# Attention with a gated MLP: score tiles by keys, one batch turned as 4-byte words on VectorE, two-bank accumulators, and the order of the work written anew

## The chip, the cores and the metric

The kernel runs on one core of a Trainium2 chip. The core has five engines that run at the same time, each through its own list of instructions in order: TensorE (PE, matrix products, which write to the PSUM accumulators), VectorE (DVE), ScalarE (ACT), GpSimd (POOL) and SyncE (SP). A weight load of the PE (PEld) overlaps its matmuls. Transfers (DMAs) run beside the engines; POOL and SP issue them. PSUM has eight banks of 2 KB for each of 128 partitions, so that one bank holds 512 fp32 columns. The metric is the time of one execution on the device, in microseconds (us), the median of several.

## The reference

Four batches of attention with eight heads, 768 positions and 64 columns a head. A query sees the 128 newest positions up to itself, and the first four positions (the sinks). The attention result, 768 x 512 per batch, goes through a gated block: a product with `w_in` and gelu give u and v of 512 columns each, v is normalised over its columns, mixed over the positions by the 768 x 768 matrix `w_sg`, and multiplied with u; a product with `w_out` is added to the attention result.

```
scores = q @ k.T / sqrt(64)
keep   = (key < 4) | ((query - key >= 0) & (query - key < 128))
x      = softmax(where(keep, scores, -1e9)) @ v          # heads side by side: (4, 768, 512)
h      = gelu(x @ w_in);  u, v = h[:, :512], h[:, 512:]
v_n    = (v - mean(v)) / sqrt(var(v) + 1e-6) * g_ln
v_s    = w_sg @ v_n + b_sg[:, None]                      # over positions, per batch
out    = x + (u * v_s) @ w_out
```

Inputs and output are fp32; the products run in bf16.

## The kernel before

Positions are cut into six tiles of 128, heads into four pairs. The whole work is a list of named steps, `STEPS`, written out in the kernel. Each step issues a few instructions; each engine carries out its own in the order of the list, and waits by semaphores for what it needs. No planner runs when the kernel is built: where a step stands in the list is what sets the order on every engine and on every DMA queue. A name carries the batch first, then a pair of heads, a tile, a half or a part, and a last letter where an engine can be chosen (A for ACT, D for DVE, P for POOL).

The steps of one batch, with their lines:

- **Loads.** Batch 0's q and k come as fp32 by SP (`LPQ`, `LPK`, L243, 384 KB each) and are cast by `CPQ`, `CPK`; those of the other batches come by POOL, cast on the way to bf16 (`LQ`, `LK`, L223, 128 KB each, six of either per batch). v comes in halves (`LVH`, L269, 384 KB), as do `w_in` (`LW`, L275, 512 KB) and `w_sg` (`LWS`, L280, 576 KB); then `w_out` (`LWO`, L283) and `b_sg` (`LB`, L299).
- **Turning q and k.** A score product needs q and k with the head's columns on the partitions. `HOW = "GBBC"` says how each batch is turned: batch 0 (G) and batches 1 and 2 (B) by PE transposes (`TQ`, `TK`, L371 and L377), read out by ACT or DVE (`EQ`, `EK`, L197, L198); batch 3 (C) by transposing DMAs from SP (`DQ`, `DK`, L435).
- **Scores.** `QK` (L478) makes one tile for a pair of heads and two tiles of queries, 2g and 2g + 1: for each of the pair's heads one matmul of 256 columns and one or two of 128, contraction 64. In a few steps of batch 0 a bias for the window is added by a matmul (L473). `EX` (L483) takes the exponential on ACT, `MK` multiplies by the window's mask on DVE (L490) or selects on POOL (L493, L496).
- **Sinks.** `KS`, `SK` and `SX` (L445, L457, L462) make the exponentials of the four sink positions, in two pieces for each batch.
- **Values.** `AV` (L519, L523, L526) makes, for one pair and two tiles (batch 0) or three tiles (the others) of queries, the products with v and with a column of ones in one PSUM bank; `NR` takes reciprocals of the sums (L535) and multiplies (L536). That is 36 such steps.
- **Block.** `XT`, `XE` (L545, L552; `XD` is the same as a DMA) turn x; `MV`, `GV` (L561, L565) make v and its gelu; `BN`, `RS`, `NM`, `Z` (L574 to L595) normalise it, where `RS` is a power on POOL (L583); `MU`, `GU` (L602, L607) make u. `WT`, `WE` (L614) turn `w_sg` once.
- **Gate and end.** `SP` (L622) multiplies with `w_sg` for one half of the positions and 128 columns, `GT` (L627) scales and adds `b_sg` on DVE, `GM` (L632) multiplies with u on DVE or POOL, `OU` (L639) multiplies with `w_out`, `RA` (L643) adds x on DVE, `ST` (L662) stores 128 rows, 24 times.

PSUM is used as two rings: two score tiles of two banks (`sc`), and four tiles of one bank (`mm`), each handed out in rotation. At the start, filler matmuls (`HM`, L188) run while the first loads come in. ACT loads a table of functions when it goes from exponentials to gelu and back.

Of the kernel before, what the change touches and what calls it, by code (L numbers as in the profile page):

```python
# [8 lines left out]
F32 = mybir.dt.float32  # L9
# [5 lines left out]
HOW = "GBBC"  # L15
VHOW = "HHHH"
# [4 lines left out]
WARM LPQ.0 FILL LPK.0 LPK.1 LPQ.1 LPQ.2 LG MASK LPK.2 LPK.3 CPQ.0.A VSK LPQ.3 IDEN CPK.0.A IDEN2 MASK0 HM.9 TQ.0.0  # L21
TK.0.0 EQ.0.0.D EK.0.0.A VSO HM.3 QK.0.0.0 ZERO CPK.1.P QK.0.0.1.1 EX.0.0.0 LVH.0.0 EX.0.0.1 QK.0.0.2.1 CPQ.1.D TK.0.1
EX.0.0.2 LC CPQ.2.D LVH.0.1 TQ.0.1 MK.0.0.0.D EK.0.1.A TQ.0.2 EQ.0.1.D EQ.0.2.A HM.2 QK.0.1.0 CPK.2.A CPK.3.P
QK.0.1.1.1 EX.0.1.0 LQ.1.0 CPQ.3.D TK.0.2 EX.0.1.1 TK.0.3 EK.0.2.D LQ.1.1 TQ.0.3 EK.0.3.A GTR EQ.0.3.D LW.0 QK.0.2.0
QK.0.2.1 EX.0.2.0 LK.1.0 KS.0 VSM.0 SK.0.2 EX.0.2.1 SK.0.1 MK.0.2.0.D AV.0.0.0 LW.1 QK.0.3.0.1 MK.0.1.0.D SX.0.1
SX.0.2 QK.0.3.1 MK.0.2.1.P GCP.D NR.0.0.0 EX.0.3.0 AV.0.0.1 AV.0.1.0 AV.0.1.1 NR.0.0.1 EX.0.3.1 QK.0.1.2 NR.0.1.0
AV.0.2.0 AV.0.3.0 EX.0.1.2 MK.0.3.1.P NR.0.1.1 QK.0.2.2 AV.0.2.1 NR.0.2.0 EX.0.2.2 TQ.1.0 NR.0.3.0 MK.0.1.2.P QK.0.3.2
AV.0.3.1 EQ.1.0.A NR.0.2.1 XT.0.0 NR.0.3.1 LWS.0 AV.0.0.2 EX.0.3.2 AV.0.1.2 XE.0.0.D LK.1.1 XT.0.1 MK.0.2.2.D MV.0.0
XE.0.1.A LK.1.2 NR.0.0.2 MK.0.3.2.D LK.1.3 NR.0.1.2 AV.0.2.2 AV.0.3.2 LQ.1.2 NR.0.2.2 GV.0.0 MV.0.1 NR.0.3.2 LQ.1.3
BN.0.0 LWS.1 XT.0.2 GV.0.1 MU.0.1 XE.0.2.A BN.0.1 WT.0 GU.0.1 TK.1.0 MV.0.2 RS.0.1 EK.1.0.A LK.1.4 NM.0.1 WE.0.A WT.1  # L30
GV.0.2 LK.1.5 TK.1.1 MU.0.2 LB.P EK.1.1.A BN.0.2 Z.0.0.A LK.2.0 WT.2 GU.0.2 MU.0.0 WE.1.D RS.0.2 WE.2.D Z.0.1.A LQ.2.0
NM.0.2 Z.0.2.A Z.0.3.D Z.0.4.D WT.3 LQ.2.1 WT.4 GU.0.0 WE.3.D WT.5 LQ.1.4 Z.0.5.D TQ.1.1 QK.1.0.0 EQ.1.1.D QK.1.1.0
# [34 lines left out]
ST.3.5  # L67
"""

HOLDS = ""


@with_exitstack
def kernel(
# [148 lines left out]
    def LQ(b, i):  # L225
        return load(q16, q, b, i)
# [484 lines left out]
```

## Time and profile before

Three runs took 156.59 to 156.99 us, median 156.65. The profiled execution has a span of 155.8 us, from its first to its last instruction, so that 0.85 us of the median lie around the span.

| | busy us | share of the span | instructions |
|---|---|---|---|
| PE, matmuls | 147.2 | 94% | 1543 |
| PEld, weight loads | 95.0 | 61% | 1543 |
| DVE | 123.0 | 79% | 295 |
| ACT | 98.9 | 63% | 110 |
| POOL | 99.7 | 64% | 127 |

Transfers moved 24.67 MB, of which the queue issued by POOL (software) moved 11.01 MB and SP's 13.41 MB. POOL's loads of batch 0's v landed 8.9 and 10.0 us after their issue, those of `w_in` 9 to 11 us; a store landed 2.3 us after its issue.

A row of the groups names line, engine and operation, output and inputs, shapes and a count, then the busy time and the mean of one in ns. The chain of work that ended last is followed back from the last instruction; a piece of it has a start, a duration and what it is. In a table by stage each row is a stretch of time. A duration in these views is that of one instruction on its engine; since matmuls are pipelined, the step from one to the next in a dense stretch of the chain is shorter than the duration of one.

### The profile page before, as it was taken

The numbers are of one execution on the slowest core, as the hardware profiler recorded it, in microseconds if no ns is written. First come the engines' busy times: TensorE is split into PE (matmuls) and PEld (weight loads), VectorE is DVE, ScalarE is ACT, GpSimd is POOL, SyncE is SP. The second block draws the span as 40 slices with busy tenths as digits, with TensorE's granted clock in tenths as the row PEclk, the third lists the DMA queues.
The fourth block names the chain that finished last, engine by engine and source line by source line (L and its number), as shares of the span: only waits on it lengthen the run. The fifth ranks groups of instructions, "written<-read, shape, count | busy, mean of one in ns | idle before, by whom it ended". The sixth has DMA issues, their size and how long they took to land.

```text
span 155.8 us, 3844 instructions
## 1 busy us (share of the span) xinstructions
PE 147.2 (94%) x1543; PEld 95.0 (61%) x1543; DVE 123.0 (79%) x295; ACT 98.9 (63%) x110; POOL 99.7 (64%) x127
## 2 busy tenths in 40 slices
PE   6998799999999999989999999999999999999990
PEld 2455487779775776747566764486567644876530
DVE  4576688829989989769789887899689956867981
ACT  3689789799989856276897855269954025591000
POOL 4099669578999899999559869640798610300400
PEclk9999689999999999999999999999999999999999
DMA  5899999999999999999999299995710580510064
GB/s 162 277 369 155 152 194 163 170 186 200 141 144 145 188 157 169 148 152 156 155 227 235 68 279 177 181 192 47 248 72 6 99 236 0 202 64 9 0 230 176
DMA packets 86170, 24.67 MB, mean 158 GB/s; under 512 B 78660, under 2 KB 83016, under 8 KB 86152
## 3 DMA queue, kind: packets, MB, share of 16 engines
q0 software_dynamic: 64608, 11.01, 97.1%
q1 hardware_dynamic: 21544, 13.41, 32.1%
q8 instruction: 12, 0.20, 0.5%
q14 instruction: 6, 0.05, 0.1%
HBM read 24.81 MB, written 6.29 MB: 200 GB/s over the span
## 4 chain that ended last, share of the span: by engine, by line
PE 75%; DMA 15%; DVE 2%; POOL 2%; issue 1%; ACT 1%; SPq 1%; ACTq 0%
PE mm L622 17%; PE sc L561 13%; PE mm L639 13%; PE sc L602 12%; DMA k<-in_k_dram 6%; DMA v_sb<-in_v_dram 6%; PE sc L478 5%; PE mm L519 4%; DMA uT<-in_k_dram 4%; PE mm L377 3%; PE mm L523 3%; PE mm L526 2%; PE mm L614 1%; PE mm L545 1%; DVE P L490 1%
## 5 line engine op out<-in xcount | busy, mean ns | idle before, releaser
L483 ACT ACTIVATE P<-sc 128x1024 bf16<-128x1024 f32 (+1 forms) x48 | 43.5, 956 | 10.9 <-PE sc L478 10.8
L622 PE MATMUL mm<-wsgT,z 128*128 128x384 bf16 x192 | 34.1, 327 | 0.0
L622 PEld LDWEIGHTS <-z 128*128 128x128 bf16 x192 | 17.7, 98 | 11.9 <-issue 0.7
L561 PE MATMUL sc<-w_in_sb,xT 128*128 128x512 bf16 x96 | 22.2, 379 | 0.7 <-ACT vt L565 0.7
L639 PE MATMUL mm<-w_out_sb,wsg_gated 128*128 128x512 bf16 x96 | 22.7, 379 | 0.0
L493 POOL TENSOR_SCALAR_AFFINE_SELECT P<-P 128x512 bf16<-128x512 bf16 x21 | 14.0, 665 | 13.3 <-ACT P L483 13.0
L627 DVE SCALAR_TENSOR_TENSOR gtmp<-mm,g_sb,b_bc 128x384 bf16<-128x384 f32 x32 | 19.1, 610 | 4.2 <-PE mm L622 3.6
L602 PE MATMUL sc<-xT,w_in_sb 128*128 128x256 bf16 x192 | 22.1, 273 | 0.0
L632 POOL TENSOR_TENSOR wsg_gated<-gtmp,uT 128x384 bf16<-128x384 bf16 x15 | 14.9, 1005 | 10.9 <-DVE gtmp L627 10.9
L574 DVE BATCH_NORM_STATS2 st<-vt 128x6 f32<-128x512 f32 x24 | 15.4, 684 | 7.5 <-ACT vt L565 7.4
L602 PEld LDWEIGHTS <-w_in_sb 128*128 128x128 bf16 x192 | 18.7, 98 | 3.0
L536 DVE TENSOR_TENSOR x_sb<-mm,rcp 128x384 bf16<-128x384 f32 (+1 forms) x36 | 18.5, 513 | 1.2
L565 ACT ACTIVATE vt<-sc 128x1024 f32<-128x1024 f32 x12 | 12.3, 1027 | 9.0 <-PE sc L561 8.9
L519 PE MATMUL mm<-v_sb,P 128*128 128x65 bf16 x192 | 16.8, 198 | 1.0 <-DMA v_sb<-in_v_dram 0.9
L643 DVE TENSOR_TENSOR ot<-mm,x_sb 128x512 f32<-128x512 f32 x24 | 16.1, 683 | 2.0 <-PE mm L639 1.9
L583 POOL TENSOR_TENSOR rs<-rs,neg_half 128x4 f32<-128x4 f32 (+1 forms) x8 | 7.0, 869 | 16.4 <-DVE rs L578 15.0
L519 PEld LDWEIGHTS <-P 128*128 128x128 bf16 x192 | 15.1, 100 | 2.9 <-issue 1.5
L223 POOL DMA_DIRECT2D q<-in_q_dram x18 | 16.7, 949 | 0.0
L223 POOL DMA_DIRECT2D k<-in_k_dram x18 | 16.4, 924 | 0.5 <-POOL wsg_gated L632 0.5
L523 PE MATMUL mm<-v_sb,P 128*128 128x65 bf16 x160 | 16.1, 197 | 0.0
L561 PEld LDWEIGHTS <-xT 128*128 128x128 bf16 x96 | 9.2, 98 | 10.9 <-issue 0.9
L478 PE MATMUL sc<-qT,kT 64*128 64x128 bf16 (+1 forms) x256 | 15.1, 242 | 0.6 <-ACT P L483 0.3
(90 smaller groups left out, 238.0 us busy)
## 6 DMA issues: line engine op xcount, KB each, us to landing
out_dram<-ot SPq DMA_DIRECT2D x24, 256.0 KB, 2.3
v_sb<-in_v_dram POOLq DMA_DIRECT2D x8, 384.0 KB, 8.5
q<-in_q_dram POOLq DMA_DIRECT2D x18, 128.0 KB, 6.3
k<-in_k_dram POOLq DMA_DIRECT2D x18, 128.0 KB, 6.5
wsg_gated<-in_moe_w_sg_dram POOLq DMA_DIRECT2D x2, 576.0 KB, 7.5
w_in_sb<-in_moe_w_in_dram POOLq DMA_DIRECT2D x2, 512.0 KB, 10.1
uT<-in_q_dram SPq DMA_DIRECT2D x2, 384.0 KB, 3.1
uT<-in_k_dram SPq DMA_DIRECT2D x2, 384.0 KB
```

The costliest lines, as they stand in the source:

```text
L223: return nc.gpsimd.dma_start(out=dst.rearrange("p (h d) -> p h d", h=H), in_=heads(src, b, i))
L478: nc.tensor.matmul(sc[:, hl, c:c + 128 * ni], at(kT, b)[rows, j, p, :], at(qT, b)[rows, i:i + ni, p, :], start=not biased, stop=(not biase ...
L483: nc.scalar.activation(out=P.new((b, p, g))[:, :, 0:w], in_=sc_ring[b, p, g][:, :, 0:w], func=AF.Exp, scale=scale)
L519: nc.tensor.matmul(av[:, il, hl, :], pt[:, hl, c:c + 128], vb[:, h, i, :], start=first, stop=False)
L523: nc.tensor.matmul(av[:, il, hl, :], pt[:, hl, c:c + 128], vb[:, h, i - 1, :], start=False, stop=(i < 2 and il == n - 1 and hl == 1))
L536: nc.vector.tensor_mul(x_sb.get(b)[:, i0:i0 + n, 128 * p:128 * (p + 1)].rearrange("p t (h d) -> p t h d", h=2), av[:, :, :, 0:Dh], rcp[:, ...
L561: nc.tensor.matmul(hp[:, jl, :], xT[b][:, 2 * g + jl, c, :], w_in_sb[:, c, d_half:2 * d_half], start=(c == 0), stop=(c == KD - 1))
L602: nc.tensor.matmul(hp[:, dc // 2, 256 * (dc % 2):256 * (dc % 2 + 1)], w_in_sb[:, c, 128 * dc:128 * (dc + 1)], xT[b][:, 2 * g:2 * g + 2, c, :],
L622: nc.tensor.matmul(ps[:, 0:NH], z[b][:, si, 128 * dc:128 * (dc + 1)], wsgT[:, si, NH * hf:NH * (hf + 1)], start=(si == 0), stop=(si == NT ...
L627: nc.vector.scalar_tensor_tensor(out=gtmp.new((b, hf, dc)), in0=mm_ring["g", b, hf, dc][:, 0:NH], scalar=g_sb[:, dc:dc + 1], in1=b_bc[:, N ...
L639: nc.tensor.matmul(ps, gated(b, hf)[:, dc, 128 * tl:128 * (tl + 1)], w_out_sb[:, dc, :], start=(dc == 0), stop=(dc == KU - 1))
L643: nc.vector.tensor_add(ot.new((b, t)), mm_ring["o", b, t], x_sb[b][:, t, :])
```

## The change

- **Score tiles by keys.** `QK` makes a tile for two tiles of keys, 2g and 2g + 1, each against its own tile of queries and the next: two matmuls of 256 columns for each head (in the last g the second has 128), instead of three. `MK`'s patterns, `wide` and the columns that `AV` reads change with it.
- **Batch 2's q and k** (`LAYOUT = "SBDM"`, letter D). They are loaded to four quarters of 32 partitions, one quarter for two heads, eight DMAs of 192 KB in place of twelve of 128 KB (`LQ.2.x` and `LK.2.x` issue two each), and turned by four 32 x 32 block transposes on DVE over 4-byte words, which hold two bf16 columns (`VQ`, `VK`). A score product then has a contraction of 32 in four groups of rows, for even and for odd columns (e), and `SK.2` is four matmuls of 512 columns. Batch 2's PE transposes and their read-out go.
- **Two-bank accumulators.** `AV` covers four heads in a tile of two banks (18 steps with one `NR` each, for 36). `SPP` and `GTP` make and read both halves of the gate for batches 0 to 2 (12 of 768 columns; batch 3 keeps eight of 384). `OUP`, `RAP` and `STP` do two row tiles of the residual at a time for batches 0 to 2, with stores of 512 KB; batch 3 keeps single rows, which it places in the q and k buffers.
- **PSUM** is eight banks, and for every ring a string `SLOTS` says which buffer each use takes.
- **`STEPS` anew.** The first pair of heads worked on is pair 2. One half of `w_sg` and nine of batch 1's twelve q and k loads come before v of batch 0, the `w_sg` transposes come early, and ten of batch 1's twelve score tiles stand ahead of the first `MV`. `LB` stands just ahead of batch 0's `RS`. There is one `SK` and one `SX` per batch, and 11 fillers instead of 14.

The instruction counts that follow: ACT's table loads 8 to 12, stores 24 to 15, `Z` on ACT 9 to 16 of 24.

```diff
-HOW = "GBBC"
+LAYOUT = "SBDM"
...
+LPK.2 ZERO WARM LPQ.2 LPQ.3 LPK.3 LWS.0 IDEN FILL LC LPK.0 LQ.1.5 CPK.2.A IDEN2 HM.9 TK.0.2 MASK CPQ.2.A HM.1 TQ.0.2
...
+LK.1.1 TK.0.0 EK.0.0.D WT.2 WE.2.D QK.0.3.2 EX.0.3.2 LQ.1.4 LQ.1.2 LVH.0.1 QK.0.3.0.1 WE.0.D LK.1.0 TQ.0.0 TK.1.2
...
+EX.1.2.0 QK.1.0.0 EX.1.0.0 LK.2.1 AV.0.0.2 NR.0.0.2 XT.0.0 LW.1 XE.0.0.D QK.1.3.2 EX.1.3.2 WT.4 WE.4.D QK.1.3.0
+EX.1.3.0 QK.1.2.2 EX.1.2.2 XT.0.2 XE.0.2.D MK.1.2.1.D SK.1 SX.1 QK.1.1.1 EX.1.1.1 QK.1.0.2 EX.1.0.2 LVH.1.1 WT.3
+MV.0.2 GV.0.2 LK.2.0 LQ.2.1 MK.1.3.2.D MK.1.3.0.D MK.1.0.0.D LG GTR GCP.D LQ.2.0 XT.0.1 XE.0.1.D VSM.1 MK.1.2.0.D
+BN.0.2 MV.0.0 GV.0.0 MK.1.3.1.P WT.5 WE.3.A BN.0.0 LK.3.0 LB.P MV.0.1 GV.0.1 WE.5.A MK.1.0.2.P RS.0.2 NM.0.2 Z.0.4.A
+BN.0.1 MK.1.2.2.P MU.0.1 Z.0.5.A MK.1.0.1.P RS.0.1 GU.0.1 AV.1.1.0 NR.1.1.0 MU.0.2 GU.0.2 NM.0.1 Z.0.2.D Z.0.1.D
+VK.2.1 Z.0.0.A MU.0.0 GU.0.0 Z.0.3.D AV.1.1.1 QK.1.1.2 NR.1.1.1 VQ.2.1 QK.1.1.0 EX.1.1.0 SPP.0.0 QK.2.1.0 EX.1.1.2
+EX.2.3.0 SPP.0.2 EX.2.2.0 VQ.2.0 GTP.0.0 LVH.1.0 VK.2.0 QK.2.0.1 MK.1.1.0.D GTP.0.2 GM.0.1.2.D LK.3.1 MK.1.1.1.P
...
+    def load(ring, src, b, x):
+        t16 = ring.get(b)
+        if LAYOUT[b] == "D":
+            for a in (2 * x, 2 * x + 1):
+                nc.gpsimd.dma_start(out=t16[32 * a:32 * a + 32].rearrange("p g (w e) -> p (g w) e", w=WK),
+                                    in_=src[b, 2 * a:2 * a + 2].rearrange("g (w i t) d -> i (g w) (t d)", w=WK, t=2))
+            return
...
+    def words(dst, ring, b, g):
+        out = dst.get(b)[:, g].rearrange("p n c -> p (n c)").bitcast(F32).rearrange("p (w i t) -> p w t i", w=WK, t=2)
+        src = ring[b][:, g].bitcast(F32).rearrange("p (w t e) -> p w t e", w=WK, t=2)
+        return nc.vector.transpose(out=out, in_=src)
+
+    def VQ(b, g):
+        words(qT, q16, b, g)
+
+    def VK(b, g):
+        words(kT, k16, b, g)
...
-        pieces = [(2 * g, 2 * g, 2, 0), (2 * g + 1, 2 * g + 1, 1, 256)] + ([(2 * g - 1, 2 * g, 1, 384)] if g else [])
-        for n, (j, i, ni, c) in enumerate(pieces):
+        for n, (j, ni, c) in enumerate(((2 * g, 2, 0), (2 * g + 1, min(2, NT - 2 * g - 1), 256))):
+            last = not biased or n == 1
+            if quad:
+                for e in range(2):
+                    for a in range(4):
+                        rows = slice(32 * a, 32 * a + 32)
+                        nc.tensor.matmul(scs[a // 2][:, a % 2, c:c + 128 * ni],
+                                         kT[b][rows, pq, 128 * j:128 * j + 128, e],
+                                         qT[b][rows, pq, 128 * j:128 * (j + ni), e],
+                                         start=(e == 0 and not biased), stop=(e == 1 and last))
+                continue
...
+    def SPP(b, dc):
+        ps = fresh(sc_ring, ("g", b, dc))
+        for hf in range(2):
+            for si in range(NT):
+                nc.tensor.matmul(ps[:, hf, 0:NH], z[b][:, si, 128 * dc:128 * (dc + 1)],
+                                 wsgT[:, si, NH * hf:NH * (hf + 1)],
+                                 start=(si == 0), stop=(si == NT - 1))
+
+    def GTP(b, dc):
+        t = gtmp.new((b, dc))
+        nc.vector.scalar_tensor_tensor(out=t, in0=sc_ring["g", b, dc][:, :, 0:NH], scalar=g_sb[:, dc:dc + 1],
+                                       in1=b_bc.rearrange("p (k s) -> p k s", k=2), op0=ALU.mult, op1=ALU.add)
...
+    def RAP(b, tp):
+        nc.vector.tensor_add(ot.new((b, tp)), sc_ring["o", b, tp], x_sb[b][:, 2 * tp:2 * tp + 2, :])
+
+    def STP(b, tp):
+        nc.sync.dma_start(out=out[b, 256 * tp:256 * (tp + 1), :].rearrange("(k p) d -> p k d", k=2), in_=ot[b, tp])
```

## The prediction

> **What bounds the kernel now.** I read the busy shares first, then the chain that ended last, then the table of busy times by stage for the first 60 us.
>
> ```profile
> span 155.8 us, 3844 instructions
> PE 147.2 (94%) x1543; PEld 95.0 (61%) x1543; DVE 123.0 (79%) x295; ACT 98.9 (63%) x110; POOL 99.7 (64%) x127
> ...
> PEclk9999689999999999999999999999999999999999
> ```
>
> ```profile
> 1.80 5.56 DMA uT<-in_k_dram
> ...
> 8.23 8.87 DMA v_sb<-in_v_dram
> 17.11 0.04 issue
> 17.15 0.33 PE mm L519 x3
> ...
> 25.23 1.73 PE sc L561 x8
> ...
> 47.62 9.45 DMA k<-in_k_dram
> 57.07 0.05 issue
> 57.12 0.40 PE mm L377 x4
> ...
> 65.31 1.19 issue
> ...
> 146.49 5.19 PE mm L639 x24
> 151.71 0.69 DVE ot L643
> ```
>
> The PE is the bound: the chain is PE for 75% of the span and DMA for 15%, nearly all of that before 57 us. Its pieces (start, duration, what) show where the PE is held: at 17.1 for v of batch 0, at 57.1 for a transfer of batch 2's k, and 1.2 us at 65.3 by a table load on ACT. From 57 us on it is almost dense.
>
> ```profile
> 0.00:5.00 5.00, 3.76 (x9) 1.20 (x9) 2.65 (x14) 2.12 (x2) 1.76 (x10) 1.00 0.55 173
> 5.00:10.00 5.00, 4.75 (x50) 2.32 (x51) 2.53 (x9) 3.33 (x4) 2.55 (x2) 1.00 0.98 342
> 10.00:15.00 5.00, 4.37 (x93) 2.87 (x92) 3.75 (x6) 5.00 (x8) 4.75 (x6) 1.00 1.97 218
> 15.00:20.00 5.00, 3.69 (x52) 2.37 (x49) 3.10 (x9) 3.96 (x7) 2.94 (x5) 0.71 3.11 157
> 20.00:25.00 5.00, 5.00 (x108) 4.42 (x106) 4.43 (x16) 4.25 (x5) 3.98 (x6) 0.95 1.42 189
> 25.00:30.00 5.00, 5.00 (x52) 3.09 (x49) 4.60 (x14) 3.89 (x4) 4.34 (x6) 1.00 1.39 165
> 30.00:35.00 5.00, 5.00 (x54) 3.88 (x52) 1.99 (x8) 4.73 (x6) 2.71 (x3) 1.00 1.95 179
> 35.00:40.00 5.00, 5.00 (x63) 4.63 (x61) 4.75 (x12) 5.00 (x7) 4.60 (x7) 1.00 1.62 193
> 40.00:45.00 5.00, 5.00 (x55) 3.20 (x52) 4.29 (x10) 4.41 (x7) 5.00 (x5) 1.00 2.13 137
> ```
>
> The columns are busy time of PE, weight load, DVE, ACT, POOL, then granted clock, DMA share and GB/s. The last column is the **supply curve**: 5 us times it, added up, gives 0.87, 2.58, 3.67, 4.45, 5.40, 6.22, 7.12, 8.08 and 8.77 MB at 5, 10, ... 45 us. As a check, the k that lands at 57.07 needs 10.35 MB of loads issued up to it; the curve (continued with 146 and 183 GB/s) has them at 54.6, and a w_in half landing at 23.50 has its bytes at 21.4. So a load lands on the curve or up to about 2.4 us after it.
>
> **The change: PE work.** Batch 2's 48 transposes go: 8 take 0.45 in the chain, so 6 x 0.45 = 2.7. Three warm-up fillers go, 0.21 each, 0.6. Batch 2's sink product becomes four 512-column matmuls: a residual group of four took 0.86 where the old sink product took 0.33, so +0.5. Score tiles keep the same columns in fewer matmuls (256 become 144 plus 96 with a contraction of 32), value, gate and output matmuls keep theirs: 0. Adding the dense chain durations of all steps gives 137.4 before, 134.5 after. If only this counted, the gain would be 2.9.
>
> For the 96 matmuls with K=32 before has no row. The nearest are the pairs with K=64, whose two matmuls start 3 ns apart and run side by side. If fours do the same, 24 sets of about 0.1 us give 2.4, as now; two at a time +2.4, one at a time +7.0. I take +0, the row's behaviour, and keep +2.4 and +7.0 for the range.
>
> **DVE, ACT, POOL, SP.** Normalising products: 24 of 557 ns and 12 of 424 become 12 of 957 and 6 of 690 (the two shapes give 158 ns + 1.04 per element), with 18 reciprocals fewer: -5.8. Gate: 32 x 610 become 12 x 1009 + 8 x 610: -2.5. Residual: 24 x 683 become 9 x 1215 + 6 x 683: -1.4. Batch 2's DVE copies go, 4 x 0.69; its four word transposes have no row: between a 128x768 cast (0.56) and two strided copies (1.9), I take one strided 128x768 copy, 0.95, so +3.8. Masks move to DVE (23 become 26, wider): +4.9; seven normalisations move to ACT (-4.0 DVE, +5.7 ACT); about six evacuations come the other way (+4.8 DVE), and the xT copies (+1.4). DVE stays near 121, ACT near 100 with four more table loads included, POOL falls by some 6 us of masks and 3.7 of issues. None of the three is the bound by its sum, so I cost these at 0: what hides them is the dense PE. Uncovered, an accumulator held 0.4 longer by its wider reader delays the next matmul: the DVE pieces of the chain are 2% (3 us) now, so -1 to +3, and I take 0. SP's stores fall from 24 to 15, and the last six of batch 3 stay single: the tail after the last matmul (155.8 - 151.5 = 4.3) is unchanged. Batch 3's six transposing transfers stay on SP, but its scores are listed 6 us of PE work sooner: four of the six must land within the 10 us listed between the first and QK.3.2.2. Those issued at 76.24 and 78.34 now land at 80.86 and 81.77, up to 4.6 each and some 1.7 apart in issue at the closest, so 4.6 + 3 x 1.7 = 9.7: just covered, 0 to +3 if their loads are late, and I take 0.
>
> Table loads go from 8 to 12. The row: ACT_TABLE_LOAD takes 1283 ns, and where one bound (65.21) the gap to the next activation was 1.3 us; four more are 5.1 us of ACT. The Trainium skill, page "ScalarE: Activation LUTs", section "What ACT_TABLE_LOAD costs", speaks against the change more strongly: about 1.38 us of drain on top, 2.66 us for each switch. By that page an estimate of the extra ACT time would be 10.6 us; the trace's 1.3 us gap does not show the drain.
>
> **The head.** This decides. Both kernels start the PE early, and the steady work that follows it is fixed, so the end is work plus **lag** (time minus PE work listed before). Before: MV.0.0 starts at 25.23 with 15.5 of work ahead of it, lag 9.8; the bound transpose at 57.12 with 45.8, lag 11.3; the end at 151.54 with 137.4, lag 14.1. After 57 us it grows by 2.8 (the table load, changes of matmul shape, some waits).
>
> The new list moves the loads. One w_sg half and nine of batch 1's twelve q, k loads stand ahead of v of batch 0 on POOL's queue, then the other three, w_sg's other half, w_in, half of batch 2's k, v of batch 1, batch 2's rest. In bytes as they land: eight fp32 loads 3.15 MB, w_sg half 0.59, nine loads 1.18, a v half 0.39: the first v half needs 5.31 MB; three loads and a v half more, 6.09; w_sg and a w_in half, 7.21; w_in, two loads of batch 2's k (0.39) and a v half, 8.52. On the curve: 24.5, 29.2, 35.5, 43.2; with 2.4 added 26.9, 31.6, 37.9, 45.6. Value products that began at 17.15 begin at 25 to 27, and the PE fills with batch 1's transposes and scores. The first MV (MV.0.2) has 21.7 of work ahead and cannot start before w_in: lag 13.8 to 16.2, where it was 9.8.
>
> Then a wait on POOL's queue. POOL's transfers run eight at a time by the built program's waits: before shows k at 52.65 issued after 0.5 idle, just behind the landing (52.12) of the v half issued eight loads earlier. In after the b_sg load, right ahead of batch 0's rsqrt, waits in this way for v of batch 1 (43.2 to 45.6). Behind it on POOL stand two narrow masks (L493's 0.66 and 0.41 for half the elements, as L326 takes for 256: 1.07 each), the rsqrt RS.0.2 (0.71), a wide mask of 1.33 and RS.0.1 (1.03): with the issue's 0.59 that is 5.8, so RS.0.1 ends at 49.0 to 51.4. Then, in line, NM 0.22, three normalisations of 0.57 on DVE and one word transpose, 2.9 together: the spatial product SPP.0.0 can go on at 51.9 to 54.3 with 35.8 ahead of it, lag 16.1 to 18.5. Behind on DVE, a normalising product (1.15), the other word transposes (3 x 0.95) and a gate (1.01) bring the first score tile of batch 2 that needs all four (39.7 of work ahead) to 56.9 to 59.3: **lag 17.2 to 19.6**.
>
> I take 17.8, below the middle: the loads of batch 2 are 8 of 192 KB rather than 12 of 128 KB, with runs twice as long, which may mend the curve a little. With the same growth of 2.8 the last matmul ends at 134.5 + 17.8 + 2.8 = 155.1; the tail 4.3 makes a span of 159.4. The profiled run of before is 155.8 against a median of 156.65, so 0.85 lies around the span: **160.3 us**, 2.3% slower. The ends of the lag give 159.7 and 162.1.
>
> The clock in the head: the 0.71 at 15 to 20 us and 0.95 after it are a half clock from 17.1 to 20.5, following the PE's gaps in the 10 to 20 us rows, about 1.7 us lost. The Trainium skill, page "TensorE: Matmul & The Clock Gate", Part 1, says the gate watches activity in windows of about 3.4 us and halves the clock after an idle one; the trace agrees (3.4 us). By that rule a longer wait in the new head would give another 1.7; no row of before can say whether the fill leaves such a gap.
>
> **The rivals.** (a) *The loads do not bind; faster.* If the early q, k, transposes and ten early score tiles fill the head, and the layer-norm on POOL is not late, the lag ends where it ends now: 134.5 + 14.1 + 4.3 + 0.85 = 153.8. For it: before binds only twice on transfers, and DMA runs below its 342 GB/s of 5 to 10 us. Against: that rate is fp32 by SP; from 15 us on, POOL's loads give 137 to 193, whatever waits. It decides if batch 2's first full score tile starts by 53.9 (lag 14.2), that is if the b_sg load's wait ends by about 40.2. (b) *Head late and more:* fours with K=32 not side by side, or wide accumulators and table loads that stall: +2.4 to +7.0, so 162.7 to 167. For it: no row of fours; against: pairs do run together. (c) *No change:* the 2.9 of PE work pays exactly for a lag between the two, 156.2 to 157.1.
>
> **How the numbers follow.** Forecast 0.55, (a) 0.25, (b) 0.14, (c) 0.06. The likeliest's own range is 157.6 to 163. The range 154.0 to 165.5 leaves out about half of (a) and the top of (b). About 0.3% tells a change of this kernel from none, so faster 0.25, same 0.06, slower 0.69.
>
> **What will show it.** Right: first value product at 25 us or later; b_sg issued after 43; RS.0.1 ending at 49 or later; first batch-2 scores after 56; chain pieces of DMA and POOL adding to over 25 us before 60; then a dense PE. Wrong: w_in landed before 33, or loads above 200 GB/s from 15 to 45 us (then (a)); K=32 matmuls starting 50 ns or more apart (then (b)); a DVE share of the chain above 5%, where the wide accumulators would be what I missed.

## The result, and the profile after

The changed kernel takes 178.38 us (177.53 to 180.51), the kernel before 156.82 us in the same comparison: a ratio of 1.135, 95% interval 1.129 to 1.141, slower. The forecast was 160.3 with a range up to 165.5: the sign is right, the size is not. The profiled execution has a span of 175.8 us against 155.8.

The head of the page of the changed kernel, with the busy shares, the busy tenths of the PE and the granted clock in 40 slices of 4.4 us:

```profile
span 175.8 us, 3648 instructions
...
PE 149.4 (85%) x1462; PEld 91.4 (52%) x1472; DVE 128.4 (73%) x248; ACT 103.1 (59%) x114; POOL 88.8 (51%) x114
...
PE   5639299899997898429989999959999999999990
...
PEclk9957969999999999975999999999999999999999
```

The PE was 94% busy and is 85% busy now; no other engine is near full. The holes lie in the first six slices (to 26 us), around 70 to 79 us (slices 17 and 18), and near 115 us (slice 27). The clock falls at 9 to 18 and 22 to 26 us, and again at 75 to 84 us.

The chain that ended last, in order of time (start, duration, what):

```profile
7.97 14.26 DMA k<-in_k_dram
22.72 1.42 PE banks L391 x24
...
33.22 9.84 DMA w_in_sb<-in_moe_w_in_dram
...
49.61 1.02 DVE nmr L604
50.63 1.20 DVE st L592 x2
...
66.76 11.09 DMA xT<-x_sb
77.89 6.59 PE banks L579 x16
...
109.30 8.41 DMA xT<-x_sb
117.75 2.76 PE banks L579 x12
```

Before, the chain was PE for 75% and DMA for 15%; now it is PE for 49%, DMA for 25% and POOL for 8%. There are two kinds of pieces. Up to 54 us it is the chain of loads and layer-norm that the prediction named. At 66.76 and 109.30 it is something that the prediction does not have: the transposing transfers of x, `XD`, of batches 1 and 2.

What the PE waited for (in total, times, longest), and the stages in which it did (busy of PE, weight load, DVE, ACT, POOL, then granted clock, DMA share, GB/s):

```profile
PE banks L579 <- DMA xT<-x_sb: 7.0, 3, 3.8
PE banks L391 <- ACT q L221: 4.0, 1, 4.0
PE banks L397 <- DMA k<-in_k_dram: 3.5, 2, 2.3
```

```profile
5.00:10.00 5.00, 2.30 (x28) 0.92 (x26) 2.56 (x5) 0.83 (x1) 4.75 (x6) 0.88 1.13 249
10.00:15.00 5.00, 3.42 (x42) 2.49 (x43) 2.37 (x4) 2.92 (x4) 0.88 (x1) 0.50 1.70 243
15.00:20.00 5.00, 3.18 (x48) 2.03 (x46) 4.39 (x7) 3.15 (x5) 1.70 (x2) 0.93 1.77 241
20.00:25.00 5.00, 3.13 (x40) 2.14 (x40) 1.97 (x3) 2.20 (x3) 4.92 (x7) 0.75 2.46 156
...
65.00:70.00 5.00, 4.57 (x54) 2.43 (x51) 3.68 (x7) 2.31 (x3) 4.93 (x6) 1.00 0.65 90
70.00:75.00 5.00, 1.85 (x7) 0.70 (x8) 3.25 (x12) 2.00 (x3) 4.67 (x5) 1.00 1.35 155
75.00:80.00 5.00, 2.10 (x5) 0.72 (x6) 2.26 (x6) 1.44 (x2) 2.80 (x4) 0.71 2.66 150
80.00:85.00 5.00, 5.00 (x16) 1.85 (x14) 1.50 (x4) 1.51 (x2) 2.03 (x3) 0.61 2.41 153
```

These three lines add to 14.5 us. Between 70 and 80 us the PE is busy for 4 of 10 us, and from 80 to 85 it is busy throughout, but at a clock of 0.61: 16 matmuls of `MV` take 6.59 us where 16 took 3.61 in the chain of before.

**Where the 20 us of span went.** Lag, as in the prediction, is the time of a step's first matmul less the PE work listed before it. Over the whole span, lag at the end less its value before is 37.1 - 14.1 = 23.0; less 2.9 of PE work, that is 20.1, the growth of the span.

| step | lag before | forecast | lag after |
|---|---|---|---|
| first `MV` | 9.6 | 13.8 to 16.2 | 19.3 (at 41.1 us) |
| SPP.0.0, first spatial product | 9.7 (SP.0.0.0) | 16.1 to 18.5 | 20.7 (56.1 us) |
| QK.2.0.1 | 12.4 | 17.2 to 19.6, taken 17.8 | 22.3 (62.0 us) |
| MV.1.2 / MV.1.0, behind `XD.1` | 12.3 / 11.5 | no growth named | 25.4 / 29.8 |
| SK.2 | 12.9 (AV.2.0.0) | no growth named | 32.4 (84.3 us) |
| MV.2.0 / MV.2.2, around `XD.2` | 13.7 / 13.7 | no growth named | 34.9 / 37.1 |
| last matmul | 14.1 | 20.6 | 37.1 |

So the head is 4.5 later than forecast, and the growth behind it is 14.8 instead of 2.8. Of that growth `XD.1` and the slow clock after it are 9.8 (22.6 at 69 us to 32.4), `XD.2` is 2.3, and 2.7 come in small steps, most of them between SK.2 and MV.2.0; from MV.2.2 to the end nothing is lost.

Times are medians of all executions; the ratios leave out the disturbed ones, among them the profiled execution of the first experiment, of which only the times are read.

### The profile page after: what moved, and what is told of

Read it like the earlier page. It is cut to its first block, busy times and chain, and to the rows that moved or that the text cites. A ratio compares the mean times of both kernels' runs of the same rounds, so it can differ in the third digit from the quotient of the medians.

```text
span 175.8 us, 3648 instructions
## 1 busy us (share of the span) xinstructions
PE 149.4 (85%) x1462; PEld 91.4 (52%) x1472; DVE 128.4 (73%) x248; ACT 103.1 (59%) x114; POOL 88.8 (51%) x114
## 4 chain that ended last, share of the span: by engine, by line
PE 49%; DMA 25%; POOL 8%; issue 6%; ACT 5%; DVE 4%; DVEq 0%; POOLq 0%
DMA xT<-x_sb 11%; PE banks L648 9%; PE banks L579 8%; DMA k<-in_k_dram 8%; PE banks L620 8%; PE banks L685 8%; DMA w_in_sb<-in_moe_w_in_dram 6%; PE banks L542 5%; PE banks L640 4%; PE banks L673 3%; ACT P L492 2%; POOL k L246 2%; PE banks L480 1%; PE banks L487 1%; POOL P L502 1%
## 5 line engine op out<-in xcount | busy, mean ns | idle before, releaser
L492 ACT ACTIVATE P<-banks 128x1024 bf16<-128x1024 f32 (+1 forms) x48 | 42.8, 952 | 11.0 <-PE banks L487 5.9
L579 PE MATMUL banks<-w_in_sb,xT 128*128 128x512 bf16 x92 | 25.0, 418 | 7.2 <-DMA xT<-x_sb 7.0
L666 POOL TENSOR_TENSOR wsg_gated<-gtmp,uT 128x384 bf16<-128x384 bf16 x14 | 13.8, 990 | 25.2 <-DVE gtmp L654 15.1
L648 PE MATMUL banks<-wsgT,z 128*128 128x384 bf16 x144 | 25.3, 326 | 0.7 <-DVE z L613 0.6
L620 PE MATMUL banks<-xT,w_in_sb 128*128 128x256 bf16 x192 | 22.4, 273 | 0.1
L583 ACT ACTIVATE vt<-banks 128x1024 f32<-128x1024 f32 x12 | 12.3, 1025 | 17.3 <-PE banks L579 17.3
L499 DVE TENSOR_TENSOR P<-P,mask 128x1024 bf16<-128x1024 bf16 (+1 forms) x26 | 19.0, 744 | 0.4 <-ACT P L492 0.4
L601 POOL TENSOR_TENSOR rs<-rs,neg_half 128x2 f32<-128x2 f32 (+1 forms) x8 | 7.7, 959 | 21.5 <-DVE rs L596 21.5
L542 PE MATMUL banks<-v_sb,P 128*128 128x65 bf16 x352 | 16.2, 193 | 0.9 <-ACT uT L625 0.9
L685 PE MATMUL banks<-w_out_sb,wsg_gated 128*128 128x512 bf16 x69 | 16.2, 379 | 0.8 <-ACT uT L625 0.7
L556 DVE TENSOR_TENSOR x_sb<-banks,rcp 128x768 bf16<-128x768 f32 (+1 forms) x18 | 15.6, 868 | 0.6
L654 DVE SCALAR_TENSOR_TENSOR gtmp<-banks,g_sb,b_bc 128x768 bf16<-128x768 f32 x12 | 12.1, 1012 | 5.1 <-PE banks L648 4.7
L610 ACT ACTIVATE z<-vt,nmr,rs 128x512 bf16<-128x512 f32 x16 | 12.1, 804 | 2.2 <-DVE nmr L604 2.1
L689 DVE TENSOR_TENSOR ot<-banks,x_sb 128x1024 f32<-128x1024 f32 x9 | 10.9, 1220 | 3.0 <-PE banks L685 3.0
```

What stands on the lines that cost most here:

```text
L492: nc.scalar.activation(out=P.new((b, p, g))[:, :, 0:w], in_=sc_ring[b, p, g][:, :, 0:w], func=AF.Exp, scale=scale)
L499: nc.vector.tensor_mul(pt[:, :, 0:w], pt[:, :, 0:w], m.unsqueeze(1).to_broadcast([128, 2, w]))
L542: nc.tensor.matmul(dst, lhsT, rhs, start=(m == 0 or jobs[m - 1][0] != bank), stop=(m + 1 == len(jobs) or jobs[m + 1][0] != bank))
L556: nc.vector.tensor_mul(rows, av[:, :, :, 0:Dh], rcp.to_broadcast([128, 2, 2 * n, Dh]))
L579: nc.tensor.matmul(hp[:, jl, :], xT[b][:, 2 * g + jl, c, :], w_in_sb[:, c, d_half:2 * d_half], start=(c == 0), stop=(c == KD - 1))
L620: nc.tensor.matmul(hp[:, dc // 2, 256 * (dc % 2):256 * (dc % 2 + 1)], w_in_sb[:, c, 128 * dc:128 * (dc + 1)], xT[b][:, 2 * g:2 * g + 2, c, :],
```

## The experiments

The forecasts call the theories by short names. On the middle: the **transposes of x** are slowed by the loads beside them, and that wait and the slow clock behind it are the loss (its rival: loads that are late of themselves); **queue**: a load put ahead of work on POOL holds that work up; **placement**: all loads of the middle can be put where neither happens. On the head: **bytes** ahead of a load set when it lands (rival: the transfers that share the channel); **layer-norm**: the wait of the `b_sg` load sets the lag. On the new forms: **slots**, how the PSUM banks are given out. Diffs of `STEPS` show only what moves.

### x of batches 1 and 2 turned by the PE

```diff
-XD.1.1 ... XD.1.0 ... XD.2.0 ... XD.2.1
+QK.2.0.0 XT.1.2 XE.1.2.A XT.1.0 XE.1.0.D XT.1.1 XE.1.1.A ...
+QK.3.2.0 EX.3.2.0 XT.2.0 XE.2.0.A XT.2.1 XE.2.1.D SPP.1.3 XT.2.2 XE.2.2.A
```

> The changed kernel with x of batches 1 and 2 turned by PE transposes and copies (as batch 0's is) instead of transposing transfers; all else as it is. Theory X (the PE's waits for the transposing transfers at 69 to 78 and 112 to 118 us, with the half clock behind the first, are a loss of their own): the time from the last score tile of batch 2's first group (starts at 69.05) to SK.2 (84.3) shrinks from 15.3 us to 7 or less, the wait at 114 goes, six PE transposes steps of 0.45 are added, and the time falls by 8 to 10 us, to about 169. Rival Y (the same time is lost a little later, on ACT, on POOL's layer-norm or on batch 3's loads): it falls by less than 4.

Measured: 170.63 us (1.087 of before, 1.081 to 1.094), 7.75 less than the changed kernel. The forecast was 8 to 10, so it fell just short, and the rival (less than 4) is out. This adds 2.7 of PE work, so that by the times 10.4 of stall went, of the 12.1 read from the lags; that is worked out, not read from a trace. The added transposes also take PSUM banks of their own. The DMA transposes of these two batches are the largest single loss of the middle.

### The loads taken away from `XD.1`

```diff
+LK.3.1 MK.1.1.1.P LWO EX.2.0.1 ... XD.1.1 ... XD.1.0 ... RS.1.2 LVH.2.0 LVH.2.1 LQ.3.2 LK.3.2 LQ.3.3 LK.3.3 LK.3.5
-LVH.2.0 ... XD.1.1 ... XD.1.0 ... LWO ... LVH.2.1 ... LQ.3.2 ... LK.3.3 LK.3.2 ... LK.3.5 LQ.3.3
+GM.1.1.3.P LVH.3.0 LVH.3.1
```

> The changed kernel with the transposing transfers of x kept, but POOL's loads moved away from them: w_out ahead of batch 1's x, v of batch 2 and five of batch 3's q, k loads behind batch 1's first layer-norm step, v of batch 3 behind the last gate of batch 1. Theory contention (the transposing transfers take 7 and 11 us because loads of POOL are in flight with them): they land 4 to 5 us after their issue, as they do before the change, the first MV of batch 1 starts by 71 and the third follows without a wait, and the time falls by 6 to 9 us. Rival lateness (x of batch 1 is finished too close ahead of its use, whatever the loads do): they still take 7 us or more, or the PE still waits 5 us or more there, and the time falls by less than 3.

Measured: 176.35 us (1.127, 1.120 to 1.135), only 2.0 better. The mechanism holds: the two transposes are issued at 65.11 and 66.65, as in the changed kernel (65.23, 66.76), but with no load in flight from 63.4 to 76.6 us `MV.1.2` starts at 69.38 and `MV.1.0` at 71.12 without a wait, where it was 72.15 and 77.89. So the first transfer takes at most 4.3 us here and 6.9 there, the second at most 4.5 and 11.1. Lag at SK.2 is 22.7, not 32.4. Then it is lost again. The PE's waits and the stages:

```profile
PE banks L620 <- DVE ot L689: 5.8, 1, 5.8
...
PE banks L542 <- DMA v_sb<-in_v_dram: 1.6, 1, 1.6
```

```profile
75.00:80.00 5.00, 4.95 (x45) 2.97 (x44) 4.93 (x16) 3.66 (x5) 4.50 (x4) 1.00 0.37 24
80.00:85.00 5.00, 3.54 (x18) 1.50 (x17) 1.35 (x2) 4.54 (x4) 5.00 (x7) 1.00 2.59 148
85.00:90.00 5.00, 2.57 (x36) 2.22 (x36) 1.91 (x1) 0.00 (x0) 4.48 (x8) 1.00 2.47 155
90.00:95.00 5.00, 0.79 (x4) 0.55 (x4) 4.93 (x9) 4.32 (x5) 2.36 (x4) 0.74 1.58 149
```

Here POOL does nothing but issue loads from 76.6 to 87.0 us, ACT is idle from 85 to 90, and the PE is busy for 0.79 of 5 us after that. v of batch 2 lands at 85.8. The layer-norm's power RS.1.1 stands behind the loads on POOL: its input is ready on DVE at 79.5, and it starts at 87.0. DVE waits for it for 6.7 us, its residual (`ot`, L689) stands behind that wait, and the PE waits 5.8 for the residual, the first line above. By QK.2.1.2 the lag is 33.2. So the forecast of 6 to 9 failed though its mechanism was right; the time is the rival's (less than 3), for another reason than the rival gave.

### The loads early, or behind the layer-norm

In the first list w_out, half of batch 1's v, v of batch 2 and one k load go behind RS.0.1, well ahead of `XD.1`; five loads of batch 3 go behind RS.1.2:

```diff
+RS.0.1 LVH.1.0 LVH.2.0 LVH.2.1 LWO LK.3.1 GU.0.1 ... RS.1.2 LQ.3.2 LK.3.2 LQ.3.3 LK.3.3 LK.3.5 ... GM.1.1.3.P LVH.3.0 LVH.3.1
```

> As the last move of loads, but v of batch 2 and w_out now right behind batch 0's layer-norm on POOL's queue, ahead of batch 1's x, where the transfers idle, and only the q, k loads of batch 3 held back behind batch 1's first layer-norm step. Theory contention plus a place for v: both of x's transfers land about 5 us after their issue, the lag stays at 22.5 to 23.5 through batch 1's MVs and at the second value product of batch 2, where the last move lost 9 us to the late v, and the time falls by 9 to 12 us against the changed kernel, to 166 to 169. Rival (the PE would wait there anyway, on batch 3's q and k or on ACT): 172 or more.

Measured: 175.0 us (171.75 to 175.79), too wide for a verdict, and above the forecast of 166 to 169; the trace is of the slowest execution. In it the lag goes through `XD.1` without a jump (25.0 at MV.1.2, 25.1 at SK.2), then from 26.2 at AV.2.0.0 to 31.7 at QK.2.1.2. POOL's own list, in order of time (start, duration), shows why:

```profile
78.97 0.97 POOL L246 DMA_DIRECT2D q<-in_q_dram  x1
79.93 0.88 POOL L246 DMA_DIRECT2D k<-in_k_dram  x1
80.80 0.89 POOL L246 DMA_DIRECT2D q<-in_q_dram  x1
81.66 1.78 POOL L246 DMA_DIRECT2D k<-in_k_dram  x2
83.39 1.81 POOL L246 DMA_DIRECT2D q<-in_q_dram  x2
85.13 0.94 POOL L246 DMA_DIRECT2D k<-in_k_dram  x1
86.02 1.11 POOL L601 TENSOR_TENSOR rs<-rs,neg_half 128x4 f32<-128x4 f32 x1
```

The power of the layer-norm (L601, RS.1.1) comes after 7 us of issues that nothing in the batch needs yet. In the second list the eight loads of batch 3 stand behind RS.1.1:

```diff
-RS.1.2 LQ.3.2 LK.3.2 LQ.3.3 LK.3.3 LK.3.5
+RS.1.1 LQ.3.2 LK.3.2 LQ.3.3 LK.3.3 LK.3.5 LQ.3.4 LQ.3.1 LK.3.4
```

> As the move of loads before (v of batch 2 and w_out early), but the eight q, k loads of batch 3 stand behind both layer-norm steps of batch 1 on POOL's queue instead of between them. Theory queue (the 5.5 us that came back between the first value product of batch 2 and its third score tile were batch 1's second layer-norm step waiting behind seven loads on POOL): that step runs by 80 instead of 86, the lag stays at 25 to 27 up to there, and the time falls by 4 to 6 us against that run. Rival (the loads of batch 3 come too late for its transposes, which then hold its scores): the lag grows again by 3 or more at batch 3's first scores, and the time falls by less than 2.

Measured: 177.32 us (1.133, 1.127 to 1.139), no better. The forecast of 4 to 6 failed and its rival came true. The layer-norm is in time now (lag 26.5 at QK.2.1.2, 27.0 at SPP.1.1), but batch 3's q and k are late, and their transposing transfers with them. The PE's waits, then two of its stages:

```profile
PE banks L487 <- DMA kT<-k: 4.6, 1, 4.6
```

```profile
95.00:100.00 5.00, 0.41 (x5) 0.13 (x4) 1.84 (x3) 0.42 (x1) 1.29 (x2) 0.75 1.37 219
100.00:105.00 5.00, 4.14 (x22) 1.77 (x20) 0.00 (x0) 1.83 (x2) 0.00 (x0) 0.57 0.91 220
```

Lag is 31.7 at QK.3.2.2 and 35.3 at MV.2.0; again a wait is followed by a low clock.

In the third list the eight are split: four early enough to land in time, none of them as a block ahead of the layer-norm.

```diff
-RS.1.1 LQ.3.2 LK.3.2 LQ.3.3 LK.3.3 LK.3.5 LQ.3.4 LQ.3.1 LK.3.4
+GM.0.0.0.P LQ.3.2 LK.3.2 LQ.3.3 LK.3.3 MV.1.2 ... RS.1.2 LK.3.5 LQ.3.4 ... RS.1.1 LQ.3.1 LK.3.4
```

> The changed kernel with v of batch 2 and w_out early (as in the queue run), and batch 3's eight loads split around the layer-norm steps of batch 1: four once x's transfers are done, two between the steps, two behind. Theory placement (each 5 to 9 us wait of the middle is one load or step in the wrong place on POOL's queue, and goes when all have a place): no PE wait over 2.5 us between 60 and 110 us, the lag at batch 3's first scores 27 to 29 instead of 33 to 34, the time 168 to 171. Rival sum (the transfers of the middle are too many for the time, whatever their order): a wait of 4 us or more comes up again somewhere before 110, and the time stays at 174 or more.

Measured: **169.77 us** (1.080, 1.074 to 1.086), 8.6 less than the changed kernel, and its wait on x is 1.1 us in all. Its chain still has the head of the changed kernel, and a shorter transpose:

```profile
7.98 14.21 DMA k<-in_k_dram
...
32.66 9.72 DMA w_in_sb<-in_moe_w_in_dram
...
66.63 5.38 DMA xT<-x_sb
72.49 4.91 PE banks L579 x22
```

The forecast (168 to 171, a lag of 27 to 29 at batch 3's first scores, no wait over 2.5 us between 60 and 110) came true: lag is 19.0 at the first `MV`s, 25.4 at SK.2, 26.9 at QK.3.2.2 and 29.8 at the end, and the longest wait is 1.6. With the same instructions, in the same order on the PE, the places of the loads alone are worth 8.6 us. The three lists before it gave 1 to 3, the second of them without a verdict: in each trace the stall came back at a later load or step.

### The wait ahead of the layer-norm of batch 0

```diff
-BN.0.0 LK.3.0 LB.P MV.0.1 ... RS.0.1 GU.0.1
+BN.0.0 MV.0.1 ... RS.0.1 LK.3.0 LB.P GU.0.1
```

> The changed kernel with the load of b_sg and one load of batch 3's k moved from ahead of batch 0's layer-norm on POOL's queue to behind it. Forecast's theory (the wait of the b_sg load for v of batch 1 holds up the layer-norm): the first RS runs at about 45.5 instead of 48.9, the second ends at about 51 instead of 53.4, the lag at the first score tiles of batch 2 falls by about 2 us and the time with it, to about 176. Rival (the vector engine's own queue, or the landing of batch 2's q at 53.3, holds the same place): the lag there falls by less than 0.7.

Measured: 176.8 us (173.58 to 179.24), too wide for a verdict; the trace is of an execution of 176.53. It shows the step: SPP.0.0 starts at 55.2 with lag 19.9 (20.7), QK.2.0.1 with 21.15 (22.3): 1.2 less where 2 were forecast and the rival had less than 0.7. RS.0.2 starts at 48.4, not at 45.5 as forecast (48.9 in the changed kernel): with the load gone, POOL waits 3.3 us for DVE's statistics, so that DVE's own list holds the place almost as late. The lag of the PE itself, 19.5 from the first `MV`s on, is a floor just under the layer-norm's. `XD.1` then takes the 1.2 back (27.5 at MV.1.2, 30.7 at SK.2). The same edit on the list with the eight loads behind RS.1.1:

> The same, with the load of b_sg and one of batch 3's k also behind batch 0's layer-norm on POOL. Theory (each wait on POOL's queue in front of a layer-norm step is on the path while the PE has nothing else): the first gate product of batch 0 starts 1 to 2 us earlier than in that run and, with no wait at x's transfers behind it, the end comes 1 to 2 us earlier too. Rival: no difference beyond 0.5.

Measured: 179.72 us (1.149, 1.143 to 1.156). Lag is 18.1 at SPP.0.0 and 18.8 at QK.2.0.1, then the earlier PE meets `XD.1` (4.9 of wait in one piece, lag 26.6) and batch 3's transposes (4.5): 37.8 at the end. SPP.0.0 starts 3.0 us earlier than without this edit (53.4 against 56.4 in a6's trace), more than forecast, and the end comes later: an earlier head did not carry through.

### The head: bytes, or who shares the channel

Batch 1's first loads are held back until a cast on POOL (`CPK.3`) is done, so that batch 0's fp32 loads have the channel to themselves; the number of bytes ahead of each later load stays.

```diff
-LC LPK.0 LQ.1.5 CPK.2.A ... CPK.3.D
+LPK.0 MASK CPK.3.P LQ.1.5 CPK.2.A ... LPQ.1 LC
```

> The changed kernel with batch 1's early q, k loads held on POOL behind a cast that waits for batch 0's fourth load, and the four small sink loads moved behind batch 0's loads on SP. Theory contention in the head (POOL's early loads share the transfers with batch 0's): batch 0's loads land by about 13 us instead of 19, the wait of the PE from 7.2 to 11.4 shrinks by 3 or more. Theory bytes (what binds the head is the sum of bytes ahead of batch 1's k and of v, in whatever order they share): the wait for batch 1's k at 18 to 22 grows by about as much, the lag at TQ.0.1 stays at 14 to 15.5 and the time within 1.5 us of the changed kernel's. If only contention counts, the lag at TQ.0.1 falls to about 11 and the time by 3 to 4 us.

Measured: 177.68 us (174.15 to 179.68), too wide for a verdict. Lag at TQ.0.1 is 14.9, where it was 14.8: the wait for batch 1's k is where it was, as the theory of bytes has it. Batch 0's last fp32 loads land at 14.7 to 16.8, where it was 14.0 to 18.9, and the PE's first wait on q did not shrink by 3: it is 4.7, where it was 4.0. So batch 1's loads, now held back, are not what makes that first wait. The half of `w_sg` is still in flight beside batch 0's loads until 11.8 here, and was not moved, so that the cause of the first wait is open.

Then the kernel before, with 1.11 MB of later loads put ahead of v of batch 0, and nothing else:

```diff
-CPK.0.A IDEN2 ... LQ.1.0 ... LQ.1.1 ... LK.1.0 ... LWS.0 ... LK.1.1
+CPK.0.A LWS.0 LQ.1.0 LK.1.0 LQ.1.1 LK.1.1 IDEN2
```

> The old kernel with one thing of the change: five of POOL's loads (one half of w_sg and the first two q and two k loads of batch 1, 1.11 MB) go ahead of v of batch 0, at 2.5 to 7 us instead of 12 to 25. Theory bytes: batch 0's fp32 loads land some 3 us later, v of batch 0 at about 22 instead of 17.1 (1.11 MB at about 200 GB/s), the lag at the first MV rises by 4 to 6 and the time to 160 to 163. Rival (the PE finds other work, or later slack takes it up): 158 or less.

Measured: 164.25 us (1.049, 1.042 to 1.056), +7.5, above the forecast of 160 to 163. Its chain in the head:

```profile
8.77 14.29 DMA v_sb<-in_v_dram
23.10 0.32 PE mm L519 x3
```

and two stages:

```profile
15.00:20.00 5.00, 2.55 (x43) 1.55 (x43) 3.06 (x5) 1.63 (x3) 2.32 (x3) 0.83 2.34 157
20.00:25.00 5.00, 2.09 (x22) 1.08 (x18) 1.75 (x6) 1.74 (x4) 1.23 (x2) 0.50 2.82 157
```

v lands at 23.1 where it landed at 17.1; 6.0 us for 1.11 MB is 185 GB/s. The PE waits for it, and its clock is at half from 20 to 25 us. Lag at MV.0.0 is 16.4 (9.6), a rise of 6.8 where 4 to 6 were forecast, at the end 21.55 (14.1): a lag of the head is kept to the end. In the changed kernel the same bytes, and another 0.66 MB of batch 1, stand ahead of v.

### A head in the old manner, with the new forms

v of batch 0 and w_in ahead of batch 1's loads, and batch 1's transposes and scores behind the first `MV`s; from SPP.0.0 on the list with the eight loads behind RS.1.1:

```diff
-LWS.0 ... nine loads of batch 1 ... LVH.0.1 ... LVH.0.0 ... LWS.1 ... LW.0 ... ten score tiles of batch 1 ... MV.0.2
+LVH.0.1 ... LVH.0.0 LW.0 ... LK.1.4 ... LW.1 ... LWS.0 MV.0.0 GV.0.0 LWS.1 ... MV.0.2 ... TQ.1.2 MU.0.1 ... QK.1.3.1
```

> The changed kernel's own steps with the head in the old manner: v of batch 0 and the v half of w_in loaded ahead of batch 1's q and k and of w_sg, which follow; batch 1's transposes between the first MVs, its scores between the gate products of batch 0; the residual of batch 0 ahead of batch 1's MVs as cover for x's transfers; POOL's loads placed as in the queue runs; buffers given out anew. Theory head (10 of the 23 us that the PE lags more are lost before the first MV by the order of the loads): the lag at the first MV is 10 to 12 instead of 19.3, at the second gate product 12 to 15 instead of 22, and the time 156 to 162. Rival (the new forms need that much early work to keep busy; with the old head they wait elsewhere): 166 or more.

Measured: 185.19 us (1.179, 1.174 to 1.185), far above the forecast of 156 to 162; the rival (166 or more) came true. The head does what it was to do: lag 12.0 at MV.0.0 (26.6 us) and 12.85 at MU.0.1, against 19.5. Then batch 2's words on DVE stand behind masks (a wait of 4.9 us for `VK`, lag 22.7 at QK.2.0.1), and the rest is worse than in the changed kernel too. With the words earlier and the loads split as above:

> The run with the old head, whose lag was 12.0 at the first MV but grew by 5 at batch 2's second score tile (a word transpose queued behind masks on VectorE) and by 12 around batch 3's transposes, with these two word transposes moved ahead of the masks and the loads placed as in the split run. Theory head plus placement: lag 16 to 18 at batch 2's second score tile (22.3 in the changed kernel), and if the middle keeps it, 20 to 26 at batch 3's first scores and a time of 160 to 168. Rival: the time stays above 172, and then the loss of the middle is not tied to how late the head is.

Measured: 182.88 us (1.164, 1.158 to 1.171); the forecast of 160 to 168 failed, the rival (above 172) came true. The PE's longest waits:

```profile
PE banks L579 <- DMA xT<-x_sb: 1.9, 2, 1.3
PE banks L212 <- DVE warm L312: 1.8, 1, 1.8
PE banks L480 <- DVE x_sb L556: 1.8, 1, 1.8
PE banks L648 <- DVE x_sb L556: 1.6, 1, 1.6
```

No wait is longer than 1.8 us; some twenty-five of 0.2 to 1.8 in the whole run, most on DVE and ACT, make the lag grow from 16.5 at 59 us to 41.4 at the end. From 60 to 100 us the PE is busy for 74% of the time, ACT for 69% and DVE for 67%, although DVE is at 85% in the first ten of these and ACT at 99% in the last: the engines wait for each other by turns. The clock has a part too: it is 0.68 from 60 to 70 us and 0.83 from 90 to 100, by (1 - clock) x 10 an estimate of 3.2 and 1.7 us. That a list with an early head and a dense middle exists for these forms was not shown; that in these two lists an early head brought nothing without such a middle was.

### The new forms in the old order

The list and head of before, batch 2 by PE transposes as before, with score tiles by keys and four-head value accumulators, gates and residuals single; the banks are given out to the one unused longest:

```diff
-HOW = "GBBC"
+LAYOUT = "SBBM"
+SLOTS: sc 246240240264026202642620... mm 010106767645401045567623...
```

> The old order of the steps with the new forms of two of them: score tiles by keys and value products of four heads in two banks (pairs merged at the place of the later one), one sink product per batch; batch 2 turned by the PE as before, gate and residual in single banks, buffers given out anew. Theory order (the loss lies in the order of the steps and loads, not in the new forms): 154 to 158.5 us, DVE busy about 6 us less than before, lag at the first MV about 10. Rival forms (tiles held longer in PSUM and in P, wide accumulators read late): 161 or more, with PE waits for DVE or ACT.

Measured: 165.41 us (1.055, 1.048 to 1.061). The head is as before (lag 10.05 at MV.0.0); 4.5 are lost between 43 and 57 us in small waits of the PE of 0.5 to 1.1 us on evacuations: on `gtmp` of DVE, and on `qT`, `kT` and `P` of ACT. The forecast (154 to 158.5) failed. With the merge a few loads, transposes and score tiles change places too. The same kernel with banks chosen for a longer distance between uses:

```diff
-sc 246240240264026202642620... mm 010106767645401045567623...
+sc 246353503502460646025151... mm 010127012723247034074305...
```

> The old order with score tiles by keys and four-head value products as in the first such run, only with PSUM banks given out so that few are taken again within six steps of their last reader (23 such places instead of 53). Theory slots (that run lost its 8 us to banks taken too soon): 156 to 160. Rival forms (the longer-held tiles and later merged value products cost it): 163 or more.

Measured: 159.62 us (1.016, 1.008 to 1.024): 5.8 less for another string of bank numbers (5.5 to 6, by medians or ratios), as forecast (156 to 160), and 2.8 over the kernel before, which is too close to 2% to be called slower. These forms in this order bring nothing, and cost 19 us less than the whole change.

## Why the prediction was right or wrong

- **PE work, -2.9: right.** Instructions and durations came as listed: the PE's list is dense from MV.2.2 to the end, with the lag constant at 37.1.
- **Fours with K=32: right.** In the row of one such group 16 matmuls of 256 columns start within 0.4 us, in four sets of four, 2 to 5 ns apart within a set and a set every 0.11 us, each with a duration of 270: four side by side. The part of rival (b) that rests on them did not happen.

```profile
L480 PE MATMUL banks<-qT,kT x16: 269/270/284, 66.4 to 66.8; 32*128 32x256 bf16 x16
```

- **DVE, ACT and POOL at 0: right in most durations, and nearly as cover.** The word transposes take 0.95 to 0.96 (taken 0.95), the wide gate and residual what their rows gave:

```profile
L654 DVE SCALAR_TENSOR_TENSOR gtmp<-banks,g_sb,b_bc 128x768 bf16<-128x768 f32 x12 | 12.1, 1012 | 5.1 <-PE banks L648 4.7
L689 DVE TENSOR_TENSOR ot<-banks,x_sb 128x1024 f32<-128x1024 f32 x9 | 10.9, 1220 | 3.0 <-PE banks L685 3.0
```

  The exception is three normalisations of batch 0 ahead of batch 2's scores, taken as 0.57 each: they took 1.43, 0.99 and 0.56. The slow two run at 53.6 to 55.9 us, while POOL issues loads (53.3 to 55.7); in a9 two took 1.43 and 1.52 beside such issues, and 0.54 without. That the issues slow them was not tested. No wait of note on a wide accumulator is among the PE's, and DVE is 4% of the chain. That batch 3's DMA transposes are "just covered" held in the changed kernel (lag 33.9 at QK.3.2.2), and a6 showed how thin that cover is.
- **Table loads: right.** Twelve of 1.283 us. Where one bounds, at 99.63, the next activation starts 1.29 us later. The Trainium skill's 2.66 us for each switch (page "ScalarE: Activation LUTs", section "What ACT_TABLE_LOAD costs") is not what this trace shows; the measured gap decides.
- **The supply curve: right, a little short.** The changed kernel moved 5.4, 7.0 and 8.8 MB by 25, 35 and 45 us, as before. The v halves landed at 27.9 and 32.9 (forecast 24.5 to 26.9 and 29.2 to 31.6), the w_in half at 38.0 (35.5 to 37.9), v of batch 1 at 47.0 (43.2 to 45.6): each 0.1 to 1.4 beyond the late end.
- **The `b_sg` wait: right as a mechanism.** Its load was issued at 47.25 after 2.75 of wait; RS.0.1 ended at 53.35, 2 beyond its range (49.0 to 51.4). The sum ran it straight behind POOL's masks; it left out that its statistics on DVE (50.55 to 52.24) stand behind a step that waits for RS.0.2, so that POOL waits for DVE. With the `b_sg` load moved the lag fell by only 1.2 at that step (a3's trace); its worth in time was not decided.
- **The head's lag, 17.8: wrong, 22.3.** The step that failed is "The first MV (MV.0.2) has 21.7 of work ahead and cannot start before w_in: lag 13.8 to 16.2". It set v, w_in and `b_sg` against the curve, and let the PE run dense up to them. It left out the first new consumer: the list has batch 1's transposes ahead of all that, and they wait for a k that lands at 22.2. That is 4.5 MB on the same curve, 20.3 to 22.7, so the page of before had it. With 7.9 of work ahead, the lag is 14.8 at TQ.0.1 already; a wait for batch 0's own fp32 q at 7 to 11 us had added 4.0 of it. Sharing the channel with batch 1's loads is not the cause of that wait (4.7 without them in a5), and what is stays open. A lag does not shrink, so w_in's landing no longer mattered: the PE came to MV.0.2 3.1 us after it. From 24 us on small steps between shapes and waits add 4.5.
- **The growth after the head, 2.8 "with the same growth": wrong, 14.8.** This is the largest error. I took the middle from before, although the change moves loads there as well, and named no cover for `XD`. Its cover is short: by a2's starts 4.3 and 4.5 us lie between the two issues and the products that need them. In the kernel before such a transfer, issued at 60.98, landed at 65.93, 4.95 later, so even at its old duration the cover would have been thin. The prediction weighed the DMA transposes of batch 3 and not those of x. The runs show 9.8 + 2.3 there; a1 (-7.75) and a9 (-8.6) take most of it back in two independent ways, and a2 beside the changed kernel shows the same two transfers without and with loads.
- **The rivals.** (a) needed batch 2's first full score tile by 53.9; it came at 62.0. (b) had the right sign and the wrong cause: neither fours, nor wide accumulators, nor tables stalled. The rival that came true, a transfer behind the head that loses its cover, was not among them.
- **The signs to look for.** Value products from 25 us, RS.0.1 after 49, batch 2's scores after 56, and over 25 us of DMA and POOL in the chain before 60 all came: the first value product is at 29.5. Of the signs of being wrong, a rate above 200 GB/s came from 15 to 20 us (241), while batch 0's fp32 loads by SP were still landing (until 18.9); after that it was 153 to 188. "Then a dense PE" did not, and that is where the 12 us are.

How the 21.6 us divide: the placement of the middle's loads is 8.6, measured; bytes ahead of v and batch 1's k in the head were measured as 7.5 in the old kernel, and the changed one has more of them; the new forms as in p2 cost 2.8. That these three add to 18.9, and the rest is the stalls that a9 still has between 55 and 110 us (lag 19 to 29.8), is a sum over different kernels and was argued, not shown.

## What to carry to other kernels

When a hand-written order moves loads, put every first consumer of every load on the supply curve in order of the list, from the first one on, and carry the lag forward: the largest early wait is a floor for all that follows. Then do the same for each transfer issued in the middle, with the loads that will be in flight beside it, and name the work that covers it; an in-order queue that issues loads and also does arithmetic has to be read as both. A load's place can be judged only with the others: three lists that moved some of them lost again at a later load what they had won, and the list that gave all of them a place won 8.6 us.

## What the runs showed of the hardware

- **A transposing transfer is slow beside loads.** The same two transposes of x landed within 4.3 and 4.5 us with no load in flight (a2), and took 6.9 and 11.1 with w_out, v and q, k loads beside them, at 150 to 155 GB/s in all from 70 to 85 us. How slow depends on the loads: beside one k load and the start of a v load such a transfer took 4.95 in the kernel before, and in a9 one took 5.4.
- **A wait of 3.8 us cost 3 more in clock.** From 77.1 to 83.9 us, over the end of the wait at 77.89, the granted clock was at half, where it was 1.00 up to 77, and 16 matmuls took 6.59 us where 16 took 3.61 before. The Trainium skill, page "TensorE: Matmul & The Clock Gate", Part 1, has a free-running window of about 3.4 us. The half clock here lasts 6.8 us, which fits two windows. I had seen this price for the head and not for a wait in the middle.
- **Bank numbers alone were worth 5.8 us** (165.4 to 159.6; 5.5 to 6), with the same instructions in the same order on every engine.
